# First head pair of the second attention set moved between the bias steps, last layer wholly in block form

## The chip, the cores and the metric

One core of one Trainium2 chip runs the whole program. The time is the device time of one execution in microseconds (us); a profile is one such execution, taken by the hardware profiler. The engines are PE (matrix products, into eight PSUM banks), DVE, ACT and POOL (element by element work; POOL reaches SBUF only) and SP, whose queue issues every DMA here.

## The reference

Attention with a bias made by a small network from positions, then a mixture of four experts over the tokens, then one more two-layer block. All is float32.

```
scores = q @ k.T / sqrt(64)                         # 2 batches, 8 heads, 576 positions
x = log1p(|i - j|) / log1p(max(i, 1))
bias = relu(x * w1 + b1) @ w2                       # 32 hidden units, 8 heads
attn = softmax(scores + bias); y = attn @ v         # tokens: 1152 x 512
out1 = sum_e p_e * (relu(y @ w1_e) @ w2_e)          # e = 0..3, 512 -> 1024 -> 512
h = out1 @ w_in; out = (h * cos(h)) @ w_out         # 512 -> 2048 -> 512
```

## The kernel before

The kernel is written as a list of steps, each with an engine, a duration, the steps it depends on and buffers by class. A planner (`Graph.order`) runs once on the host: it takes the steps in the order of their priorities as engines and buffers come free in its own count of time, and so fixes the order of every engine's queue. On the chip each queue then runs strictly in that order, and an instruction waits by semaphore only for the data and the buffers that it needs. The priorities are the order of writing, shifted by offsets (`O_...`) and by a list of seeds, `MOVES`; `P_...` say how much later an alternative engine may take a step.

Buffer classes that matter here: E (14 tiles of 128x640, named es: keys, values and scores of the first set, bias rows, score tiles), F (fs, 128x512), K (ks, split keys, queries and values), P1 (four single PSUM banks, p_153 to p_156) and P2 (two pairs of PSUM banks, p_160 and p_161).

The stages, in the order of writing:

- **Bias.** 36 steps (`bias_step`), each for 16 query positions and all 8 heads. Four operations on DVE or ACT make the hidden values (line 495 or 493), PE reduces them (line 506), DVE or ACT takes the result out (513 or 511), and SP stores it in DRAM (`biasD`), for steps of the mirrored part in a reversed copy too (line 524 on ACT, 525 on POOL; `biasR`). A step is 384, 448, 512 or 576 columns wide; one of 576 takes a P2 pair, the others a P1 bank.
- **First set** (`first_set`), the first 64 query positions, after four bias steps: for each head pair p = 0..3 and each batch b keys and values are loaded into E tiles, PE makes the scores (line 663), DVE adds the bias row and takes the minimum (617), ACT the exponential (620), POOL normalises (630), PE transposes (647, 650) and multiplies with the values (672).
- **Second set** (`second_set`), the other 512 positions, written after all 36 bias steps. Here products are split in a high and a low float32r part. `prep_pair` loads keys, queries and values of a pair and splits them: the high part on POOL or ACT (lines 538, 539), the low part on POOL or DVE (540). Each score product (line 699, 12 matmuls) fills both P2 pairs, one for each head; two minima, exponentials and normalisations follow, transposes, and products with the values (719). A pair p has four parts: two halves g of the positions by two batches, each with two score products. The bias tile of a score product is loaded from DRAM and serves both batches.
- **Fill** (`fill`, lines 1026, 1034): expert layers on the first 128 tokens, which the planner puts between the steps of the second set.
- **Experts** on the other 1024 tokens, mostly in block form (`block_products`, line 907): each 2x2 block product of 8 products is done with 7, on sums of blocks that DVE makes before. Token sums (`block_tokens`) are made of tokens that were stored in DRAM (`x1D`, `x2D`) and loaded again. Second layers are line 786, transposes of the result line 996.
- **Last layer**, in four chunks c of 512 hidden units. With `PLAIN = 1` chunk 0 is done directly (line 777) for all 1152 tokens, chunks 1 to 3 directly for the first 384 and in block form for the other 768. Its weights are split into parts during the expert stage (`singles`, `quads`), stored in DRAM and loaded again.

Of the kernel before, what the change touches and what calls it, by code (L numbers as in the profile page):

```python
# [36 lines left out]
    2173958, 2074786, 2643280, 8547416, 3098374, 2108113, 823829, 3486615, 5170615, 9452828,  # L37
    2633387, 6676825, 3992994,
# [234 lines left out]
def t_pool(n, ptr=0, two=False):  # L273
    return 145 + n * (2.11 if two else 0.86) + 80 * ptr
# [20 lines left out]
Q1 = S - Q0  # L295
# [8 lines left out]
NCONV, LATE, PLAIN = 2, 3, 1  # L304
# [5 lines left out]
NWAIT = 8  # L310
# [5 lines left out]
P_GEN, P_ADD, P_SPA, P_SPD, P_E32, P_REL, P_SUB, P_NRM, P_EV, P_REV, P_TWO = 200.0, 2500.0, 150.0, 1500.0, 300.0, 300.0, 2000.0, 3000.0, 3000.0, 50.0, 0.0  # L316

ON_ACT, P_HDV, P_HAC, P_EVD = ((36, (2, 3)),), 300.0, 150.0, 200.0

O_GEN, O_SGN, O_STT, O_ADD, O_SPL, O_EVC, O_NRM = 80, 80, -150, 0, 150, -10, 0  # L320

BAHEAD, HAHEAD, FAHEAD, BACK, BACK0, G_SET, G_FILL, G_MAIN = 7, 3, 2, 4, 2, 33, 6, 1
# [42 lines left out]
def build(ctx: ExitStack, tc: tile.TileContext, consts, q, v, qd, kp, vp, w12, probs, mw1, mw2, win, wout, out):  # L365
# [111 lines left out]
    bias_st, bias_mm = [], {}  # L477

    def bias_step(s, back, p2, gates=()):
# [9 lines left out]
        for t in range(4):  # L489
# [8 lines left out]
            G.step(*first, rd=rdt, wr=[(hid[t // 2], t)], after=gate, off=O_SGN if t in ts else O_GEN, port=True, alts=[(*other, wait)])  # L498
# [12 lines left out]
        G.step("ACT", t_act(W, 1), lambda: nc.scalar.activation(out=uo(), in_=pi(), func=AF.Copy, scale=nrec[:, s:s + 1]),  # L511
# [21 lines left out]
    x1_st, x2_st = {}, {}  # L533
    n_units = [0]
# [23 lines left out]
    def prep_pair(b, p, gate):  # L558

        kf, qf = Buf("E"), Buf("F")  # L560
        KH, KL, QH, QL = Buf("K"), Buf("K"), Buf("K"), Buf("K")
        dma(128 * S * 4, lambda: nc.sync.dma_start(out=kf.tile[:, :S], in_=kp[b, p]), wr=[kf], after=gate)
# [50 lines left out]
    def unit(bt, sp, es, i, out, tail, used):  # L613
# [3 lines left out]
        low = G.step("DVE", t_dve(S) + 10, lambda: nc.vector.tensor_tensor_reduce(  # L617
# [8 lines left out]
        G.step("DVE", 80, lambda: nc.vector.reciprocal(out=stats[:, 3, c:c + 1], in_=stats[:, 2, c:c + 1]), rd=[(st, "t")], wr=[(st, "r")])  # L626
# [56 lines left out]
    def second_set(p, gates):  # L683
# [3 lines left out]
        for g, b in ((g, b) for g in range(2) for b in range(B)):  # L687
# [15 lines left out]
            for hh in range(2):  # L703
# [20 lines left out]
                G.step("DVE", t_dve(256) + 40, lambda bank=bank, xt=xt, m0=m0, g=g, x32=x32: nc.vector.tensor_tensor(  # L724
# [3 lines left out]
            if g:  # L728
                whole(p, b, x32)

    def whole(p, b, x32):
        cs = slice(B * Q0 + Q1 * b, B * Q0 + Q1 * b + Q1)
        x1_st[p, b] = dma(128 * Q1 * 4, lambda: nc.sync.dma_start(out=x1D[p, :, Q1 * b:Q1 * b + Q1], in_=x32.tile[:, :Q1]), rd=[x32])
        G.step("ACT", t_act(Q1, 0, 1), lambda: nc.scalar.activation(out=xh[:, p, cs], in_=x32.tile[:, :Q1], func=AF.Copy),
               rd=[x32], wr=[(fix("xh"), (p, b))])
        sub = lambda e: e.tensor_tensor(out=xl[:, p, cs], in0=x32.tile[:, :Q1], in1=xh[:, p, cs].bitcast(F32), op=ALU.subtract)
        G.step("POOL", t_pool(Q1, 0, True), lambda: sub(nc.gpsimd), rd=[x32, (fix("xh"), (p, b))], wr=[(fix("xl"), (p, b))],
               alts=[("DVE", t_dve(Q1), lambda: sub(nc.vector), P_SUB)], port=True)
# [4 lines left out]
    for b, qs in enumerate(qss):  # L743
        dma(128 * 512 * 4, lambda b=b, qs=qs: nc.sync.dma_start(out=qs.tile[:, 0:512], in_=qd[b]), wr=[qs], after=[bias_mm[b, 0]])
# [43 lines left out]
    def run_ff(jobs, evac1, evac2, xr, final=None):  # L788
# [28 lines left out]
        l2(*todo.pop(0))  # L817
# [8 lines left out]
    def block_tokens(cols, keys, n, whole, stored, after, names=("xh", "xl"), t4n="t4"):  # L826
# [4 lines left out]
        def block(d):  # L831
            def load(dd, c):
                b = Buf("F")
# [19 lines left out]
            two(v22, v22, v12, ALU.subtract, [b22, b12], [b22], n, after=x)  # L853
            keep_("T2", v22, b22)

            two(v21, v21, v22, ALU.subtract, [b21, b22], [b21], n)
# [39 lines left out]
    def block_products(A, T_, n, evac, mid=None):  # L896
# [56 lines left out]
    def block_job(e, f0, cols, T_, n, gate, last):  # L953
# [3 lines left out]
        hbs = block_products(A, T_, n, moe_ev1)  # L957
# [382 lines left out]
```

## Time and profile before

| | |
|---|---|
| three runs, median (lowest to highest) | 778.99 us (778.15 to 780.88) |
| profiled execution: its time / its span | 780.83 / 779.0 us |
| PE busy | 761.4 us (98%), 4310 matmuls |
| DVE / ACT / POOL busy | 633.9 / 452.3 / 127.7 us |
| mean granted clock of PE | 0.989 |

The span runs from the first to the last instruction. PE's busy time counts a matmul from its start to the modelled end, so that overlapping ones make a full row even when each is slow. The granted clock says which share of full speed PE had.

### The profile page before, as it was taken

Reading aid. Unit: us, or ns where it says so; the run is one execution under the profiler, and the core shown is the slowest. Engines: PE = TensorE matmul, PEld = TensorE weight load, DVE = VectorE, ACT = ScalarE, POOL = GpSimd, SP = SyncE. Lnnn points to the kernel's source line nnn. Section 1 sums busy time; section 2 is a strip of 40 time slices with the busy share of each in tenths; the row PEclk is TensorE's granted clock in tenths of the full one; section 3 lists DMA queues with packets and bytes.
Section 4 is the critical chain, followed back from the end, with each engine's and each line's share of the span. In section 5 each row is a group of like instructions: output and inputs, shape, how many; then the busy total and the mean of one; then the engine's idle time right before and its main releaser. Section 6 shows DMA issues by size and latency. Waiting matters only on the chain.

```text
span 779.0 us, 13118 instructions
## 1 busy us (share of the span) xinstructions
PE 761.4 (98%) x4310; PEld 624.8 (80%) x4310; DVE 633.9 (81%) x1507; ACT 452.3 (58%) x950; POOL 127.7 (16%) x177
## 2 busy tenths in 40 slices
PE   9898799999999999999999999999999999999998
PEld 5445687887877888888888888888889899999987
DVE  7895687888786986979697979899979959986573
ACT  8885687878776545354445544544547647564440
POOL 0134575756637000000000000000000000000000
PEclk9999699999999999999999999999999999999999
DMA  6799966676728336162615644627594578462212
GB/s 196 234 302 296 300 206 220 193 237 198 232 60 288 133 121 213 49 201 79 229 42 162 218 148 136 211 99 231 187 302 147 185 267 286 151 221 82 77 59 95
DMA packets 94516, 142.00 MB, mean 182 GB/s; under 512 B 11505, under 2 KB 42865, under 8 KB 94449
## 3 DMA queue, kind: packets, MB, share of 16 engines
q1 hardware_dynamic: 94448, 141.17, 55.9%
q8 instruction: 34, 0.56, 0.3%
q14 instruction: 34, 0.27, 0.1%
HBM read 101.05 MB, written 40.08 MB: 181 GB/s over the span
## 4 chain that ended last, share of the span: by engine, by line
PE 76%; DVE 1%; ACT 1%; issue 0%
PE p L786 23%; PE p L907 18%; PE p1x L786 12%; PE p L777 7%; PE p1x L907 5%; PE p1x L777 3%; PE p L719 2%; PE p L1034 2%; PE p L647 1%; PE p L1026 1%; PE p L699 1%; PE p L996 1%; PE p1x L1026 0%; DVE ht L712 0%; DVE es L617 0%; DVE hs L551 0%
## 5 line engine op out<-in xcount | busy, mean ns | idle before, releaser
L786 PE MATMUL p<-wx,hs 128*128 128x512 f32 x804 | 188.5, 390 | 0.0
L786 PEld LDWEIGHTS p<-wx,hs 128*128 128x128 f32 x804 | 150.3, 188 | 31.2
L786 PE MATMUL p1x<-wx,hs 128*128 128x512 f32 (+1 forms) x408 | 93.9, 383 | 0.0
L786 PEld LDWEIGHTS p1x<-wx,hs 128*128 128x128 f32 x408 | 75.0, 188 | 14.8
L630 POOL TENSOR_SCALAR es<-es,stats 128x576 f32<-128x576 f32 (+2 forms) x104 | 64.7, 637 | 71.4 <-DVE stats L626 22.8
L907 PE MATMUL p<-xh,wx 128*128 128x512 f32 (+1 forms) x236 | 76.4, 374 | 0.0
L907 PE MATMUL p<-tx,wx 128*128 128x512 f32 (+1 forms) x294 | 69.4, 373 | 0.0
L620 ACT ACTIVATE es<-es,stats 128x576 f32<-128x576 f32 x72 | 55.4, 770 | 15.7 <-DVE stats L617 15.0
L617 DVE CUSTOM_DVE_ANT_0 es<-p,es 128x576 f32<-128x576 f32 x72 | 52.6, 750 | 12.3 <-DMA es<-biasD 5.5
L907 PEld LDWEIGHTS p<-tx,wx 128*128 128x128 f32 x294 | 54.1, 188 | 8.2
L539 ACT ACTIVATE wx<-fs 128x512 fp32r<-128x512 f32 (+1 forms) x71 | 41.2, 600 | 26.2 <-DVE fs L823 20.2
L540 DVE TENSOR_TENSOR wx<-fs,wx 128x512 fp32r<-128x512 f32 (+1 forms) x67 | 44.2, 676 | 12.7 <-ACT wx L539 12.5
L551 DVE TENSOR_TENSOR hs<-p,hs 128x512 fp32r<-128x512 f32 x64 | 43.5, 688 | 10.2 <-ACT hs L549 9.1
L777 PE MATMUL p<-xh,wx 128*128 128x384 f32 (+1 forms) x184 | 51.5, 351 | 0.0
L647 PEld LDWEIGHTS p<-ident,es 128*128 128x128 f32 x288 | 34.0, 145 | 20.0 <-issue 9.2
L647 PE MATMUL p<-ident,es 128*128 128x128 f32 x288 | 46.1, 287 | 3.7 <-POOL es L630 2.8
L907 PEld LDWEIGHTS p<-xh,wx 128*128 128x128 f32 x236 | 44.0, 188 | 6.8
L987 DVE SCALAR_TENSOR_TENSOR fs<-p,prob,fs 128x512 f32<-128x512 f32 x47 | 35.0, 745 | 17.2 <-PE p L786 15.5
L907 PE MATMUL p<-xl,wx 128*128 128x512 f32 (+1 forms) x118 | 44.2, 374 | 0.0
L495 DVE TENSOR_SCALAR bs<-cst,cpos 128x576 f32<-128x576 f32 (+3 forms) x98 | 41.7, 487 | 1.4 <-PE p L506 1.2
L699 PE MATMUL p<-ks,ks 64*128 64x288 f32 x384 | 36.1, 322 | 6.6 <-DVE stats L617 5.0
L539 ACT ACTIVATE fs<-fs 128x256 fp32r<-128x256 f32 x45 | 18.4, 415 | 40.3 <-DVE fs L1098 40.1
(198 smaller groups left out, 1544.5 us busy)
## 6 DMA issues: line engine op xcount, KB each, us to landing
fs<-in_mw SPq DMA_DIRECT2D x113, 256.0 KB, 4.2
wx<-winhl SPq DMA_DIRECT2D x32, 256.0 KB, 4.8
wx<-wouthl SPq DMA_DIRECT2D x32, 256.0 KB, 4.5
wouthl<-fs SPq DMA_DIRECT2D x23, 256.0 KB, 2.4
winhl<-fs SPq DMA_DIRECT2D x22, 256.0 KB, 2.6
fs<-in_wout SPq DMA_DIRECT2D x22, 256.0 KB, 3.5
fs<-in_win SPq DMA_DIRECT2D x20, 256.0 KB, 3.9
es<-in_kp SPq DMA_DIRECT2D x16, 288.0 KB, 4.6
```

What stands on the lines that cost most here:

```text
L495: dve = ("DVE", t_dve(W, 1, True), lambda w0=w0, u=u, t=t: nc.vector.tensor_scalar(out=hv(t), in0=tab[:, w0:w0 + W], scalar1=cpos[:, u:u + ...
L539: act = ("ACT", t_act(n, 0, 1), lambda: nc.scalar.activation(out=hv(), in_=fv(), func=AF.Copy))
L540: low = lambda e: e.tensor_tensor(out=lv(), in0=fv(), in1=hv().bitcast(F32), op=ALU.subtract)
L551: G.step("DVE", t_dve(n) + 25, lambda: nc.vector.tensor_tensor(out=dst(AL), in0=src(), in1=dst(AH).bitcast(F32), op=ALU.subtract), rd=[ps_ ...
L617: low = G.step("DVE", t_dve(S) + 10, lambda: nc.vector.tensor_tensor_reduce(out=f3(e.tile[:, :S]), in0=sp.tile[:, :, 0:288], in1=f3(bt.til ...
L620: exp_all.append(G.step("ACT", t_act(S, 1, 1) + 124, lambda: nc.scalar.activation(out=e.tile[:, :S], in_=e.tile[:, :S], func=AF.Exp, scale ...
L630: nrm = lambda g: g.tensor_scalar(out=dst(), in0=src(), scalar1=rs, scalar2=1.0, op0=ALU.mult, op1=ALU.mult)
L647: nc.tensor.transpose(tp.tile[:, 128 * kt:128 * kt + 128], e.tile[:, 128 * kt:128 * kt + 128], ident)
L699: nc.tensor.matmul(out=o[hh], lhsT=x.tile[ls, c:c + 128], rhs=y.tile[ls, cols], start=(i == 0), stop=(i == 2))
L777: nc.tensor.matmul(out=z.tile[:, 0:n], lhsT=w[dt][2][wi]()[:, 128 * ft:128 * ft + 128], rhs=x[:, dt, p0:p0 + n], start=(dt == 0 and i == 0 ...
L786: nc.tensor.matmul(out=y.tile[:, 0:m], lhsT=hx, rhs=w[ft][2][wi]()[:, c0:c0 + m], start=(ft == 0 and i == 0), stop=(ft == nf - 1 and i == 2))
L907: nc.tensor.matmul(out=z.tile[:, 0:n], lhsT=x()[:, 128 * t:128 * t + 128], rhs=y(), start=(start and d == 0 and i == 0), stop=(d == 1 and ...
```

## The change

- **Order of writing.** The first pair's second set (p = 0) is now begun after 24 bias steps: `second_set` became a generator that stops after each of its four parts, `BIAS_AT = 24, 30, 36` puts its first part behind step 24, the second behind step 30 and the third behind step 36.
- **Keys and values.** The first set takes the pairs in the order 1, 2, 3, 0, and the E tiles of pair 0 are kept (`raw`), so that `prep_pair` splits them from there. Two loads of keys and four of values go away; the values' tile has another layout, which the splits read with a stride. The first loads of the first set wait for the first hidden values only (`EARLY`).
- **Last layer.** `PLAIN = 0`: chunk 0 too is done directly for 384 tokens and in block form for 768. Its weights now also need the block sums (stores and loads of `s12`, `s34`). The experts' second layers end with token tiles 3, 4, 1, 2 and no longer in falling order; the parts of tiles 6 to 8 that only the direct form read are no longer written.
- **The planner's numbers.** New seeds, offsets, waits and a few durations; more of the hidden values go to ACT (59 instead of 46), fewer to DVE (85 instead of 98).
- New branches for `NHALF = 0` are not taken (`NHALF = 1`), and `direct` stays empty.

```
 MOVES = (
-    2173958, 2074786, 2643280, 8547416, 3098374, 2108113, 823829, 3486615, 5170615, 9452828,
...
+    7995270, 9512881, 659327, 8807516, 3479167, 4347581, 5230207, 3159208, 2587635, 4906331,
...
-NCONV, LATE, PLAIN = 2, 3, 1
+NCONV, LATE, PLAIN = 2, 3, 0
...
-NWAIT = 8
+NWAIT = 4
+
+SHARE, EARLY, QEARLY = 1, 1, 0
+
+BIAS_AT = 24, 30, 36
...
-ON_ACT, P_HDV, P_HAC, P_EVD = ((36, (2, 3)),), 300.0, 150.0, 200.0
...
+ON_ACT, P_HDV, P_HAC, P_EVD = ((8, (2, 3)), (36, (3,))), 50.0, 50.0, 200.0
...
     def prep_pair(b, p, gate):
 
-        kf, qf = Buf("E"), Buf("F")
+        had = raw.get((p, b))
+        kf, qf = had[0] if had else Buf("E"), Buf("F")
         KH, KL, QH, QL = Buf("K"), Buf("K"), Buf("K"), Buf("K")
-        dma(128 * S * 4, lambda: nc.sync.dma_start(out=kf.tile[:, :S], in_=kp[b, p]), wr=[kf], after=gate)
+        if not had:
+            dma(128 * S * 4, lambda: nc.sync.dma_start(out=kf.tile[:, :S], in_=kp[b, p]), wr=[kf], after=gate)
...
-            vf, V = Buf("F"), Buf("K")
+            vf, V = had[1] if had else Buf("F"), Buf("K")
...
         kf, vf, at, bank = Buf("E"), Buf("E"), Buf("E"), Buf("P1")
+        if p < SHARE:
+            raw[p, b] = kf, vf
...
             head_end.append(qk_all[-1])
             if g:
                 whole(p, b, x32)
+            yield
...
-    for p in range(4):
+    for p in (*range(SHARE, 4), *range(SHARE)):
         shared = None
         for b in range(B):
-            shared = first_set(p, b, qss[b], [bias_mm[NSTEP0 - 2, 0]] + head_end[-FAHEAD:1 - FAHEAD], shared)
+            gate = hid0[:1] if len(head_end) < EARLY else [bias_mm[NSTEP0 - 2, 0]]
+            shared = first_set(p, b, qss[b], gate + head_end[-FAHEAD:1 - FAHEAD], shared)
...
-    for s in range(NSTEP0, 36):
-        bias_step(s, BACK, False)
+    made = NSTEP0
     for p in range(4):
-        second_set(p, [bias_mm[G_SET, 0]])
+        for n in BIAS_AT if p == 0 else ():
+            while made < n:
+                bias_step(made, BACK, False)
+                made += 1
+            if n == BIAS_AT[0]:
+                parts = second_set(p, [bias_mm[G_SET, 0]])
+            next(parts)
+        for _ in parts if p == 0 else second_set(p, [bias_mm[G_SET, 0]]):
+            pass
...
-            for j in range(n // 128) if c or not last else reversed(range(n // 128)):
+            for j in range(n // 128) if c or not last else reversed(range(n // 128)) if PLAIN else (2, 3, 0, 1):
...
+            d0 = 2 if t >= 6 and not PLAIN else 0
```

PE's queue where the first set ends and the second begins. Before: the last transposes and value product of the first set (lines 647, 650, 672) are followed at once by score products of the second set (line 699), all bias steps being done.

```order
L506 MATMUL p_161<-bs_146,prm 32x288 x2
L672 MATMUL p_155<-es_131,es_139 128x128 x5
L647 MATMUL p_153<-ident,es_129 128x128 x4
L650 MATMUL p_156<-ident,es_129 64x128
L672 MATMUL p_156<-es_129,es_142 128x128 x5
L699 MATMUL p_161<-ks_117,ks_119 128x288
L699 MATMUL p_160<-ks_117,ks_119 128x288
...
L699 MATMUL p_160<-ks_118,ks_119 128x288
L699 MATMUL p_161<-ks_118,ks_119 128x288
L647 MATMUL p_156<-ident,es_142 128x128 x4
```

After, at the same place (the same operations are now lines 657, 660, 684, 711 and, for the bias, 512; 1058 is the fill's first layer):

```order
L657 MATMUL p_155<-ident,es_136 128x128 x4
L660 MATMUL p_154<-ident,es_136 64x128
L684 MATMUL p_153<-es_142,es_129 128x128 x5
L684 MATMUL p_154<-es_132,es_135 128x128 x5
L711 MATMUL p_161<-ks_117,ks_125 128x288
...
L512 MATMUL p_154<-bs_147,prm 32x448 x2
...
L512 MATMUL p_160<-bs_151,prm 32x288 x2
...
L512 MATMUL p_155<-bs_147,prm 32x448 x2
...
L1058 MATMUL p_154<-x_80,fs_98 128x128
L711 MATMUL p_161<-ks_117,ks_125 128x288
```

Eleven bias steps have moved behind the first score product: four of 448 columns and seven of 576 (printed as 288, in two halves). Eight of them, and the fill's first layer, stand before the second score product, the last three before the third.

POOL's queue at the splits of pair 0. Before, they (lines 538, 540) follow the last normalisation of the first set (line 630):

```order
L630 TENSOR_SCALAR es_131<-es_131,stats 128x576
L630 TENSOR_SCALAR es_129<-es_129,stats 128x576
L538 TENSOR_SCALAR ks_117<-es_137 128x576
L540 TENSOR_TENSOR ks_118<-es_137,ks_117 128x576
L538 TENSOR_SCALAR ks_119<-fs_99 128x512
```

After, they (lines 544, 546) stand among normalisations (line 640) and reversed copies (531):

```order
L640 TENSOR_SCALAR es_140<-es_140,stats 128x576
L544 TENSOR_SCALAR ks_117<-es_136 128x576
L544 TENSOR_SCALAR ks_119<-es_129 128x5x64
L546 TENSOR_TENSOR ks_118<-es_136,ks_117 128x576
L640 TENSOR_SCALAR es_142<-es_142,stats 128x576
L640 TENSOR_SCALAR es_132<-es_132,stats 128x576
L546 TENSOR_TENSOR ks_120<-es_129,ks_120 128x5x64
L531 TENSOR_SCALAR fs_101<-es_141 128x222
```

From the first normalisation to the last split of a query, POOL has 24 instructions in the new order: 8 normalisations, 4 splits of keys (2 high, 2 low) and 12 shorter ones.

PE's queue where the last layer begins. Before, the last transposes of the experts' result (line 996) are followed by the direct products of chunk 0 (line 777), 96 in all:

```order
L996 MATMUL p_153<-ident,fs_111 128x128 x4
L777 MATMUL p_154<-xh,wx_3160 128x384
...
L996 MATMUL p_153<-ident,fx_2854 128x128 x4
L777 MATMUL p_156<-xh,wx_3160 128x384
```

After (transposes 1026, block products 937, direct products 803):

```order
L1026 MATMUL p_155<-ident,fs_112 128x128 x4
...
L1026 MATMUL p_155<-ident,fs_113 128x128 x4
L937 MATMUL p1x_2710<-xh,wx_2750 128x384
...
L1026 MATMUL p_153<-ident,fs_109 128x128 x4
L937 MATMUL p_156<-xh,wx_2750 128x384
...
L803 MATMUL p_153<-xh,wx_2750 128x384
...
L937 MATMUL p_153<-tx_2991,wx_3151 128x384
```

Eighteen block products that read tokens directly, and 48 direct ones, now stand between the last transposes of a blocked tile and the first block product that reads a token sum (tx).

## Rows read from the trace of the kernel before

**Rows 1.** The head of the page, and PE's part of its first section.

```profile
span 779.0 us, 13118 instructions
...
PE 761.4 (98%) x4310; PEld 624.8 (80%) x4310; DVE 633.9 (81%) x1507; ACT 452.3 (58%) x950; POOL 127.7 (16%) x177
```

**Rows 2.** Busy time by stretches: length, engines, granted clock, DMA share, GB/s.

```profile
25.00:35.00 10.00, 7.20 (x54) 3.86 (x54) 7.34 (x22) 8.02 (x17) 2.45 (x4) 0.83 0.62 204
70.00:75.00 5.00, 4.36 (x37) 3.08 (x29) 1.25 (x5) 1.56 (x3) 3.11 (x4) 1.00 0.86 274
75.00:80.00 5.00, 1.74 (x13) 1.17 (x12) 0.23 (x1) 2.01 (x5) 4.24 (x6) 0.74 0.93 290
80.00:85.00 5.00, 2.29 (x15) 2.02 (x16) 2.85 (x9) 2.40 (x6) 3.63 (x4) 0.50 0.92 281
85.00:90.00 5.00, 4.36 (x25) 3.71 (x24) 3.85 (x14) 3.02 (x7) 1.73 (x3) 0.50 0.83 295
90.00:95.00 5.00, 5.00 (x44) 4.55 (x45) 3.75 (x14) 3.33 (x10) 2.96 (x6) 0.90 0.92 263
95.00:250.00 155.00, 152.52 (x1198) 125.28 (x1195) 126.24 (x363) 120.18 (x272) 98.85 (x137) 1.00 0.65 205
256.00:776.00 520.00, 519.99 (x2444) 446.37 (x2443) 430.95 (x938) 259.62 (x529) 0.00 (x0) 1.00 0.49 160
```

**Rows 3.** PE in order of time: start, length, instructions, idle before and releaser.

```profile
29.96 1.12 PE L647 MATMUL p<-ident,es 128*128 128x128 f32 x4 [2.80 <-POOL es L630]
...
48.14 1.71 PE L506 MATMUL p<-bs,prm 128*32 128x448 f32 x16
...
60.38 2.15 PE L506 MATMUL p<-bs,prm 128*32 128x288 f32 x32
...
73.43 1.57 PE L672 MATMUL p<-es,es 128*128 128x128 f32 x10 [0.64 <-ACT es L555]
75.39 0.40 PE L699 MATMUL p<-ks,ks 64*128 64x288 f32 x2 [0.39 <-POOL ks L538]
77.05 1.33 PE L699 MATMUL p<-ks,ks 64*128 64x288 f32 x10 [1.25 <-POOL ks L540]
82.71 1.81 PE L699 MATMUL p<-ks,ks 64*128 64x288 f32 x12 [4.33 <-DVE stats L617]
```

**Rows 4.** DVE in order of time: first minimum, a run of hidden values, second set.

```profile
26.33 0.76 DVE L617 CUSTOM_DVE_ANT_0 es<-p,es 128x576 f32<-128x576 f32 x1 [1.54 <-DMA biasD<-es]
...
52.06 2.64 DVE L495 TENSOR_SCALAR bs<-cst,cpos 128x576 f32<-128x576 f32 x6
...
81.01 0.76 DVE L617 CUSTOM_DVE_ANT_0 es<-p,es 128x576 f32<-128x576 f32 x1 [5.49 <-DMA es<-biasD]
```

**Rows 5.** POOL in order of time: normalisations, then the splits of the keys.

```profile
29.15 1.58 POOL L630 TENSOR_SCALAR es<-es,stats 128x576 f32<-128x576 f32 x2
...
52.33 2.98 POOL L630 TENSOR_SCALAR es<-es,stats 128x576 f32<-128x576 f32 x1 [0.28 <-ACT bs L493]
...
66.67 0.75 POOL L630 TENSOR_SCALAR es<-es,stats 128x576 f32<-128x576 f32 x1 [6.95 <-DVE stats L626]
...
72.20 0.68 POOL L538 TENSOR_SCALAR ks<-es 128x576 fp32r<-128x576 f32 x1 [0.52 <-DMA es<-in_kp]
72.96 1.40 POOL L540 TENSOR_TENSOR ks<-es,ks 128x576 fp32r<-128x576 f32 x1
```

**Rows 6.** DMA issues from 60 to 82 us: count, size, median us to landing.

```profile
es<-in_kp SPq DMA_DIRECT2D x2, 288.0 KB, 4.4
...
es<-biasD SPq DMA_DIRECT2D x2, 256.0 KB, 4.8
```

**Rows 7.** The chain that ended last: start, length, pieces; last layer.

```profile
582.71 0.44 PE p L996 x4
...
641.55 2.08 PE p L907 x12
```

**Rows 8.** DMA issues from 560 to 600 us, the tokens stored and loaded again.

```profile
x2D<-fs SPq DMA_DIRECT2D x6, 256.0 KB, 2.8
...
fs<-x2D SPq DMA_DIRECT2D x5, 192.0 KB, 3.6
```

More of the change, by code (lines that the diff above doesn't have):

```diff
@@ L273, in t_pool @@
 def t_pool(n, ptr=0, two=False):
-    return 145 + n * (2.11 if two else 0.86) + 80 * ptr
+    return (170 if two else 145) + n * (2.11 if two else 0.86) + 90 * ptr
 def t_col(n):
@@ L497, in bias_step @@
             first, other, wait = (act, dve, P_HDV) if t in ts else (dve, act, P_HAC)
-            G.step(*first, rd=rdt, wr=[(hid[t // 2], t)], after=gate, off=O_SGN if t in ts else O_GEN, port=True, alts=[(*other, wait)])
+            x = G.step(*first, rd=rdt, wr=[(hid[t // 2], t)], after=gate, off=O_SGN if t in ts else O_GEN, port=True, alts=[(*other, wait)])
+            hid0.append(x)
         pb = Buf("P1" if npc == 1 else "P2")
@@ L510, in bias_step @@
         pi = lambda: pb.tile[:, :, 0:m] if npc == 2 else pb.tile[:, 0:m]
-        G.step("ACT", t_act(W, 1), lambda: nc.scalar.activation(out=uo(), in_=pi(), func=AF.Copy, scale=nrec[:, s:s + 1]),
+        G.step("ACT", t_act(W, 1) + 20, lambda: nc.scalar.activation(out=uo(), in_=pi(), func=AF.Copy, scale=nrec[:, s:s + 1]),
                rd=[pb, (cb, "r1")], wr=[(u_, 0)], off=O_STT,
@@ L616, in unit @@
         n_units[0] += 1
-        low = G.step("DVE", t_dve(S) + 10, lambda: nc.vector.tensor_tensor_reduce(
+        low = G.step("DVE", t_dve(S) + 25, lambda: nc.vector.tensor_tensor_reduce(
             out=f3(e.tile[:, :S]), in0=sp.tile[:, :, 0:288], in1=f3(bt.tile[:, :S]), scale=-0.125, scalar=BIG,
@@ L824, in two, with block_tokens @@
         return G.step("DVE", t_dve(n), lambda: f(nc.vector), rd=rd, wr=wr, port=True, **kw)
-    def block_tokens(cols, keys, n, whole, stored, after, names=("xh", "xl"), t4n="t4"):
+    def block_tokens(cols, keys, n, whole, stored, after, names=("xh", "xl"), t4n="t4", had={}):
         c0, c1 = cols
@@ L832, in load @@
             def load(dd, c):
+                if (dd, c) in had:
+                    b = had[dd, c][0]
+                    return b, (lambda: b.tile[:, 0:n])
                 b = Buf("F")
@@ L998, in moe_ev2 @@
             cs = slice(128 * t, 128 * t + 128)
-            G.step("ACT", t_act(512), lambda: nc.scalar.activation(out=xh[:, :, cs], in_=f3(tp.tile, 4), func=AF.Copy),
+            d0 = 2 if t >= 6 and not PLAIN else 0
+            m = 128 * (4 - d0)
+            G.step("ACT", t_act(m), lambda: nc.scalar.activation(out=xh[:, d0:4, cs], in_=f3(tp.tile, 4)[:, d0:4], func=AF.Copy),
                    rd=[tp], wr=[(fix("x2h"), t)])
@@ L1004, in moe_ev2 @@
                     out=x2D[:, :, 128 * t - 384:128 * t - 256].rearrange("a p n -> p a n"), in_=f3(a(), 4)), rd=[acc[t]])
-            G.step("DVE", t_dve(512), lambda: nc.vector.tensor_tensor(
-                out=xl[:, :, cs], in0=f3(tp.tile, 4), in1=xh[:, :, cs].bitcast(F32), op=ALU.subtract),
+            G.step("DVE", t_dve(m), lambda: nc.vector.tensor_tensor(
+                out=xl[:, d0:4, cs], in0=f3(tp.tile, 4)[:, d0:4], in1=xh[:, d0:4, cs].bitcast(F32), op=ALU.subtract),
                 rd=[tp, (fix("x2h"), t)], wr=[(fix("x2l"), t)])
```

63 lines of the change are left out of this document (36 added, 27 removed).

## The prediction

> **What bounds the kernel now.** I read the head of the page first: PE is busy 761.4 of 779.0 us [rows 1], so whatever shortens the kernel must either fill PE's holes or take work from PE. The table by stretches shows where which holds [rows 2]. From 256 us on PE is busy 519.99 of 520 us at a granted clock of 1.00: nothing gets faster there except by fewer matmuls. From 95 to 250 us it is busy 152.52 of 155. Ahead of that lie two holes. Busy time times granted clock is the time that the same work would take at full speed; by that measure the stretch from 25 to 35 us does 7.20 x 0.83 = 6.0 us of work in 10 and loses 4.0 us. The five stretches from 70 to 95 do 4.36 + 1.29 + 1.15 + 2.18 + 4.50 = 13.5 us of work in 25 and lose 11.5 us. Of these 11.5, 7.2 us are idle time (25 minus 17.75 busy) and 4.3 us are matmuls at the lower of the two clock levels (1.2 instead of 2.4 GHz), where the clock fell after PE had been idle and stayed through 80 to 90. Each us of idle time cost about 0.6 us more in clock.
>
> PE's instructions in order of time say what the holes wait for [rows 3]. In the first, transposes of the first set wait 2.80 us for POOL's normalisation; behind that stands DVE's first minimum, which had waited 1.54 us for a DMA [rows 4]. The second begins at 75.0 (73.43 + 1.57), when the first set and the bias are finished. The first score products of the second set wait 0.39 and 1.25 us for the splits, which POOL started at 72.20 when the keys landed: 0.68 + 1.40 us [rows 5]. Then PE waits 4.33 us for DVE's minimum, since the two PSUM pairs are full, and that minimum waits 5.49 us, until 81.01, for its bias tile from DRAM [rows 4]. The tile's load takes 4.8 us [rows 6] while the DMA engines are 0.92 to 0.93 busy [rows 2]. So the second hole is a pipeline that starts cold: load, split, product, load, minimum, with nothing else for PE to do.
>
> **The change, term by term.** The sum is made against the profiled execution, 780.83 us (span 779.0 and 1.83 around it). The median of the runs is 778.99, 1.84 lower; I carry the difference over unchanged.
>
> *Cover for the second hole.* Eleven bias steps now stand behind the first score product. Two steps of 448 columns take 1.71 us, two of 576 take 2.15 [rows 3]: 4 x 0.855 + 7 x 1.075 = 10.9 us of PE work, placed where PE waits today, against a hole of 11.5 us. It is the same work as before, so what is gained is the hole, not the work. The keys and values of the first part need no load: two loads of 288 KB and four of 160 KB go, 1.2 MB, or 4.2 us of DMA at the 290 GB/s of 75 to 80 us. At best both holes vanish: -15.5 us. From this I subtract new waits.
>
> - *First hole.* It has the same cause, and the new order only puts another score product and bias step ahead of the transposes and issues the first loads earlier. Bounds: 0.5 us (a few short waits) to 4.0 (unchanged). I take 2.
> - *Splits in time.* PE reaches the first score product of the second set about 10.9 us earlier, and 2 us earlier again for the first hole: 75.0 - 12.9 = 62. POOL by then must have done 24 instructions from its first normalisation at 29.15: 8 normalisations of 0.75 = 6.0, four key splits 2 x (0.68 + 1.40) = 4.2, 12 shorter ones at about 0.5 (between 0.2 and 0.7, scaled by columns from 0.68) = 6.0; together 16.2 us, with 33 us to do them in [rows 5]. Yet where DVE ran six hidden-value operations in a row (52.06 to 54.70 [rows 4]), a normalisation took 2.98 us instead of 0.75 [rows 5]. DVE has 37 such operations in that time, 37 x 2.64/6 = 16.3 us at most. If the two engines exclude each other altogether, the end is 29.15 + 16.2 + 16.3 = 61.7, just PE's 62. Bounds 0 and 5 us; I take 1.
> - *Second bias tile.* The E tile for the second score product's bias row comes free only at the last transposes of the first set, and its load takes 4.8 us [rows 6]; bias steps of 576 columns then miss the held PSUM pair. Bounds 0 and 3, taken 1.5, since eight bias steps lie between.
> - *DVE between the first and third score product.* It still makes hidden values there, against some 11 us of bias work and two score products of about 2 us on PE. Bounds 0 and 4 (the 4.33 wait), taken 1.
> - *Bias tiles of the last steps.* A store and a load stand between the last bias steps and the minima that read them, 2.8 and 4.8 us by the nearest rows [rows 6, 8]; bounds 0 and 3, taken 1.
> - *Clock.* Only a long idle piece costs it; bounds 0 and 3, taken 0.
>
> New waits: 2 + 1 + 1.5 + 1 + 1 = 6.5. First part: -15.5 + 6.5 = -9.0 us.
>
> *Last layer.* Chunk 0 in block form needs 36 products more on token sums, 32 fewer on xh and 16 fewer on xl: 12 matmuls of 384 columns fewer, and twelve take 2.08 us [rows 7]. That is paid in full, where PE is never idle: -2.1.
>
> *Its start.* Before, 96 direct products covered the way of the last experts' tokens through DRAM; now the first product on a token sum comes earlier. Between the transposes of the last blocked tile and that product PE has a second-layer group (12 x 512 columns, 2.08 x 512/384 = 2.8), two transposes (0.44 each [rows 7]), 18 block products (3.1) and 48 direct ones (8.3): 15.1 us. The way: store 2.8, load 3.6 [rows 8], and about five DVE or ACT operations no longer than the 0.76 of a minimum [rows 4]: 10.2. Slack 5; bounds of the wait 0 and 3, taken 0.3. The sums `s12` and `s34` add 16 transfers of about 256 KB and some 26 operations on DVE, hidden by a DMA share of 0.49 and by DVE's 431 of 520 us [rows 2]; without that cover the transfers alone would cost 4.2 MB at 160 GB/s, 26 us.
>
> *95 to 250 us.* The second set's other pairs are reordered by the seeds alone; 2.5 us are idle there, so 0, between -2 and +2.
>
> Sum: -9.0 - 2.1 + 0.3 = -10.8; 780.83 - 10.8 = 770.0 for an execution like the profiled one, 768.2 for the median.
>
> **Rivals.**
>
> *Nearly all of it comes back (762).* Every new wait at its low bound: -15.5 + 0.5 - 2.1 = -17.1. For it: 10.9 us of cover against 11.5 of loss, and the splits no longer wait for a load. Against it: five waits at their bounds at once.
>
> *The shared port (775).* POOL's splits lag behind DVE's hidden values, by the 2.98 for 0.75 us. The first score product is then 5 us late instead of 1, and the clock falls for 3 us: -10.8 + 4 + 3 = -3.8. Against it: DVE makes fewer hidden values than before (85 operations, not 98), and POOL has 33 us for 16. The Trainium skill, "SBUF — State Buffer", section "SBUF: two separate sides", says that DVE and GpSimd share a pair of ports as an exclusive lock, held for one whole instruction. By that rule a POOL instruction would wait at most for the one DVE operation in progress, 0.44 us here, some 10 us over 24 instructions, and the splits would be in time. The trace agrees that one blocks the other; the row is harsher than the rule: the normalisation waited out a run of operations, not one.
>
> *Bound by DMA, the hole only moves (777).* In 70 to 95 us the DMA engines are 0.83 to 0.93 busy, and only 1.2 MB (4.2 us) leaves. Were the bias tiles late for that reason in the new order as well, 4.2 of the 11.5 us and the 2.1 of the last layer would come back, and waits at the interleaved steps of some 4 us would eat most of it: 777. Against it: the transfers now spread over a longer stretch, since the bias stores no longer end before the second set begins.
>
> *Slower (784).* PE's queue is strict: the first score product of the second set stands ahead of eleven bias steps that were ready without it. If it is late, they all are; each us is paid in full, with 0.6 on top when the clock falls as it did after 75 us. The forecast's 10.8 is eaten, and 2.3 us beyond, at (10.8 + 2.3)/1.6 = 8 us of lateness more, i.e. if POOL's 16.2 us and the DVE work that excludes it stretch by a quarter (32.5 to 41). At 10 us: -10.8 + 16 = +5. For it: a row in which POOL took four times its time. Against it: it would have to be so for most of the stretch.
>
> **Numbers.** Forecast (764 to 773) 0.55; nearly all back 0.20; shared port 0.12; bound by DMA 0.07; slower 0.06. 0.3%, or 2.3 us, is about what runs of this kernel can tell from no change. Faster: 0.55 + 0.20 + 0.12 = 0.87; same 0.07; slower 0.06. The range 760 to 777 leaves out the last case, half of the one bound by DMA and about 0.05 below; the likeliest case's own is 764 to 773.
>
> **What would show it.** Right: PE starts the first second-set score product (now line 711) near 62 us, has no wait over 2 us from 60 to 95, and the granted clock is 1.00 there; 12 matmuls of 384 columns fewer; the first product on a token sum (937) waits under 0.5 us. Wrong: a wait of line 711 for POOL of several us with the clock falling behind it; a wait of DVE's minimum for biasD as long as the 5.49; a hole at the start of the last layer; or a first hole as wide as before.

## The result and the profile after

The changed kernel takes 765.69 us (median of 4 runs, 765.42 to 766.26); the kernel before took 779.36 in the same comparison (4 runs). The ratio is 0.9825, interval 0.9806 to 0.9843: 13.7 us faster. The forecast was 768.2, in a range of 760 to 777. The profiled execution takes 765.42 us, its span is 763.6. It lies 0.27 us below its median, where the one of before lies 1.5 above its own, so the two traces differ by 1.7 us more than the medians do.

The head of the page and PE's part of its first section, to hold against [rows 1]:

```profile
span 763.6 us, 13117 instructions
...
PE 754.7 (99%) x4298; PEld 619.9 (81%) x4298; DVE 644.9 (84%) x1520; ACT 457.2 (60%) x962; POOL 124.7 (16%) x180
```

There are 12 matmuls fewer, and PE is idle 8.9 us instead of 17.6. The same stretches as in [rows 2], with length, PE, PEld, DVE, ACT, POOL, granted clock, DMA share and GB/s:

```profile
25.00:35.00 10.00, 9.71 (x81) 6.62 (x73) 7.32 (x23) 7.92 (x21) 3.37 (x6) 1.00 0.75 248
70.00:75.00 5.00, 4.37 (x43) 3.46 (x36) 3.97 (x12) 4.03 (x8) 2.21 (x4) 1.00 0.71 258
75.00:80.00 5.00, 5.00 (x62) 3.35 (x63) 4.31 (x11) 4.84 (x11) 1.71 (x3) 1.00 0.96 310
80.00:85.00 5.00, 5.00 (x51) 4.21 (x43) 2.29 (x6) 2.50 (x6) 0.00 (x0) 1.00 0.95 306
85.00:90.00 5.00, 5.00 (x25) 2.65 (x25) 3.84 (x14) 2.88 (x8) 1.73 (x3) 1.00 0.89 302
90.00:95.00 5.00, 5.00 (x45) 4.30 (x45) 4.35 (x13) 3.24 (x8) 1.86 (x4) 1.00 0.90 299
95.00:250.00 155.00, 153.45 (x1173) 126.85 (x1172) 135.96 (x372) 122.69 (x277) 94.56 (x130) 1.00 0.65 206
256.00:760.00 504.00, 504.00 (x2371) 432.99 (x2370) 424.81 (x925) 255.01 (x524) 0.00 (x0) 1.00 0.52 172
```

Both holes are gone, and the clock stays at its higher level throughout. Counted as in the prediction (length less busy time times granted clock), 25 to 35 us now loses 0.3 us instead of 4.0, 70 to 95 loses 0.6 instead of 11.5, and 95 to 250 loses 1.6 instead of 2.5.

PE in order of time where the second set begins, to hold against [rows 3]:

```profile
59.52 1.03 PE L711 MATMUL p<-ks,ks 64*128 64x288 f32 x11
60.48 5.52 PE L512 MATMUL p<-bs,prm 128*32 128x448 f32 x54
66.28 0.94 PE L512 MATMUL p<-bs,prm 128*32 128x448 f32 x2 [0.28 <-DVE bs L500]
67.63 2.90 PE L512 MATMUL p<-bs,prm 128*32 128x288 f32 x40 [0.42 <-ACT es L517]
70.46 1.16 PE L1058 MATMUL p<-x,fs 128*128 128x128 f32 x8
72.25 1.06 PE L711 MATMUL p<-ks,ks 64*128 64x288 f32 x12 [0.63 <-DVE es L519]
...
73.74 1.06 PE L1058 MATMUL p<-x,fs 128*128 128x128 f32 x8
...
78.51 1.06 PE L1058 MATMUL p<-x,fs 128*128 128x128 f32 x8
79.49 1.18 PE L512 MATMUL p<-bs,prm 128*32 128x288 f32 x16
80.60 1.16 PE L1058 MATMUL p<-x,fs 128*128 128x128 f32 x8
...
84.93 1.98 PE L1066 MATMUL p<-fs,fs 128*128 128x512 f32 x4
86.85 1.07 PE L711 MATMUL p<-ks,ks 64*128 64x288 f32 x12
87.84 1.12 PE L1066 MATMUL p<-fs,fs 128*128 128x512 f32 x2
```

The first score product runs from 59.3 to 60.5, and the waits behind it are 0.28, 0.42 and 0.63 us. But the reader should see a second kind of work between the score products, which the prediction did not price: the fill's two layers (lines 1058 and 1066). From 70 to 95 us they take 6.4 + 4.1 = 10.5 us of PE; before, the fill had 2.75 us there.

The DMA issues from 45 to 70 us say where its weights come from (size, count, median us to landing). After, and below it before:

```profile
fs<-in_mw SPq DMA_DIRECT2D x6, 256.0 KB, 4.4
...
fs<-in_q SPq DMA_DIRECT2D x2, 256.0 KB, 2.9
```

```profile
es<-in_kp SPq DMA_DIRECT2D x4, 288.0 KB, 4.6
es<-in_vp SPq DMA_DIRECT2D x3, 320.0 KB, 4.5
```

After, six loads of fill weights (in_mw) have been issued by 70 us; before, none, and DMA was still busy with keys and values, all but one of these loads being the first set's.

DVE's first minimum and POOL's normalisations among the splits, to hold against [rows 4, 5]:

```profile
22.13 0.75 DVE L627 CUSTOM_DVE_ANT_0 es<-p,es 128x576 f32<-128x576 f32 x1
```

```profile
47.31 0.87 POOL L544 TENSOR_SCALAR ks<-es 128x576 fp32r<-128x576 f32 x1 [0.99 <-DMA es<-in_kp]
48.26 1.41 POOL L546 TENSOR_TENSOR ks<-es,ks 128x576 fp32r<-128x576 f32 x1
...
52.19 1.07 POOL L640 TENSOR_SCALAR es<-es,stats 128x576 f32<-128x576 f32 x1 [0.21 <-DVE stats L636]
...
54.71 1.39 POOL L544 TENSOR_SCALAR ks<-fs 128x512 fp32r<-128x512 f32 x2 [0.42 <-DMA fs<-in_q]
```

The first minimum no longer waits and comes 4.2 us earlier. The last key split ends at 49.7 and the last query split at 56.1, 3 us before PE needs them.

### The profile page after: what moved, and what is told of

The parts are those of the page before. It is cut to its first block, busy times and chain, and to the rows that moved or that the text cites. A ratio compares the mean times of both kernels' runs of the same rounds, so it can differ in the third digit from the quotient of the medians.

```text
span 763.6 us, 13117 instructions
## 1 busy us (share of the span) xinstructions
PE 754.7 (99%) x4298; PEld 619.9 (81%) x4298; DVE 644.9 (84%) x1520; ACT 457.2 (60%) x962; POOL 124.7 (16%) x180
## 4 chain that ended last, share of the span: by engine, by line
PE 90%; DVE 4%; ACT 2%; DMA 2%; issue 1%; POOL 0%; SPq 0%; DVEq 0%; ACTq 0%
PE p L812 22%; PE p L937 19%; PE p1x L812 14%; PE p1x L937 7%; PE p L803 5%; PE p L731 4%; PE p L711 4%; PE p L657 4%; PE p L1066 4%; PE p L1058 3%; DVE bs L500 3%; PE p1x L803 2%; PE p L512 1%; DMA biasD<-es 1%; PE p L684 1%
## 5 line engine op out<-in xcount | busy, mean ns | idle before, releaser
L812 PE MATMUL p<-wx,hs 128*128 128x512 f32 (+1 forms) x756 | 177.0, 387 | 0.0
L812 PEld LDWEIGHTS p<-wx,hs 128*128 128x128 f32 x756 | 140.1, 188 | 28.2
L812 PE MATMUL p1x<-wx,hs 128*128 128x512 f32 x456 | 109.8, 390 | 0.0
L812 PEld LDWEIGHTS p1x<-wx,hs 128*128 128x128 f32 x456 | 85.4, 188 | 17.6
L937 PE MATMUL p<-xh,wx 128*128 128x512 f32 (+1 forms) x252 | 80.5, 371 | 0.0
L555 ACT ACTIVATE hs<-p 128x512 fp32r<-128x512 f32 x62 | 35.9, 593 | 9.2 <-PE p L657 8.5
L512 PE MATMUL p<-bs,prm 128*32 128x288 f32 (+3 forms) x384 | 39.6, 486 | 1.8 <-DVE bs L500 0.9
L498 ACT ACTIVATE bs<-cst,cpos 128x576 f32<-128x576 f32 (+3 forms) x59 | 37.9, 700 | 2.2 <-DVE cst L465 1.9
L803 PE MATMUL p<-xh,wx 128*128 128x384 f32 (+1 forms) x128 | 37.5, 356 | 0.0
L731 PE MATMUL p<-hs,ks 128*128 128x256 f32 x248 | 36.9, 293 | 0.5 <-DVE ht L724 0.5
```

The lines of the kernel that those rows point to most:

```text
L498: act = ("ACT", t_act(W, 1, 1), lambda w0=w0, u=u, t=t: nc.scalar.activation(out=hv(t), in_=tab[:, w0:w0 + W], func=AF.Relu, bias=cpos[:, ...
L512: nc.tensor.matmul(out=pv(a)[32 * t:32 * t + 32], lhsT=wpad, rhs=hv(t, m * a, m), start=True, stop=True, tile_position=(0, 32 * t))
L731: nc.tensor.matmul(out=bank.tile[:, 256:512], lhsT=V.tile[:, 128 * kt:128 * kt + 128], rhs=m, start=(i == 0), stop=(i == 8))
L803: nc.tensor.matmul(out=z.tile[:, 0:n], lhsT=w[dt][2][wi]()[:, 128 * ft:128 * ft + 128], rhs=x[:, dt, p0:p0 + n], start=(dt == 0 and i == 0 ...
L812: nc.tensor.matmul(out=y.tile[:, 0:m], lhsT=hx, rhs=w[ft][2][wi]()[:, c0:c0 + m], start=(ft == 0 and i == 0), stop=(ft == nf - 1 and i == 2))
L937: nc.tensor.matmul(out=z.tile[:, 0:n], lhsT=x()[:, 128 * t:128 * t + 128], rhs=y(), start=(start and d == 0 and i == 0), stop=(d == 1 and ...
```

## The experiments

All medians are set against the kernel before on the same chip. "Lost" is PE time lost from 60 to 95 us, worked out as above from seven windows; "fill" is the PE time of the fill's two layers from 70 to 95 us; "weights" is the number of fill weight loads issued from 45 to 70 us.

| run | median us | ratio, interval | lost | fill | weights |
|---|---|---|---|---|---|
| before | 779 | 1 | 11.5 | 2.8 | 0 |
| changed | 765.7 | 0.983 (0.981 to 0.984) | 1.4 | 10.5 | 6 |
| changed, again | 766.0 | 0.984 (0.982 to 0.986) | 1.2 | 10.5 | 6 |
| changed, chunk 0 done directly | 771.1 | 0.989 (0.987 to 0.991) | 1.6 | 9.6 | 6 |
| bias steps first | 769.4 | 0.987 (0.985 to 0.989) | 3.8 | 9.1 | 4 |
| keys and values loaded again | 771.8 | 0.990 (0.988 to 0.993) | 5.1 | 4.3 | 0 |
| both of the last two | 774.3 | 0.993 (0.991 to 0.995) | 8.1 | 1.1 | 0 |
| EARLY = 0 | 774.1 | 0.995 (0.994 to 0.997) | 5.5 | 3.0 | 0 |
| fill held back | 777.5 | 0.998 (0.997 to 1.000) | 7.8 | 0 | 0 |
| fill held back, bias steps first | 777.9 | 0.999 (0.998 to 1.000) | 11.6 | 0 | 0 |
| before, fill's first weights early | 786.1 | 1.008 (1.006 to 1.010) | 11.8 | 9.5 | 8 |
| before, two groups' weights early | 796.6 | 1.022 (1.020 to 1.024) | 11.0 | 10.5 | 8 |
| changed, no seeds | 773.0 | 0.992 (0.990 to 0.995) | 5.5 | 3.6 | 0 |
| changed, fill's first weights early | 768.5 | 0.986 (0.984 to 0.987) | 3.8 | 6.4 | 8 |

**Chunk 0 done directly again.**

```diff
-NCONV, LATE, PLAIN = 2, 3, 0
+NCONV, LATE, PLAIN = 2, 3, 1
```

> The changed kernel with chunk 0 of the last layer done directly again (PLAIN = 1); all queues up to the experts are as in the changed kernel. Theory: the block form pays its 12 matmuls in full, so this kernel is 2.1 us slower than the changed one, 767.8 us, or 767.5 if the start of the last layer waits 0.3 us in block form. Rival: the start of the block form, or its extra sums and transfers, give it back; then 765.7, the same as the changed kernel.

Measured: 771.12 us (0.989, 0.987 to 0.991), 5.1 more than the changed kernel's repetition: neither of the two that were expected. The stretches say why. It has 12 matmuls more, and PE is idle for 1.88 us between 250 and 550, where it waits twice for DVE and ACT at a block product:

```profile
PE p L937 <- ACT fs L944: 1.0, 1, 1.0
PE p L937 <- DVE fs L947: 0.9, 1, 0.9
```

That is a part whose queues differ from the changed kernel's. The first 25 us lost 3.6 us instead of 1.3, in the same order on every engine; the two traces' first minima are at 23.81 and 22.13. So the 2.1 us of the 12 matmuls, taken from their price and not measured alone, are one of three pieces of the 5.1, and the two others belong to the experts' order and to the start; the difference of the medians alone does not measure the block form.

**Bias steps first; keys and values loaded again; both.**

```diff
-BIAS_AT = 24, 30, 36
+BIAS_AT = 36,
```

```diff
-SHARE, EARLY, QEARLY = 1, 1, 0
+SHARE, EARLY, QEARLY = 0, 1, 0
```

> The changed kernel with the second set begun only after all 36 bias steps (BIAS_AT = 36); the first pair's keys and values are still kept from the first set. Theory (the bias steps are cover for a cold pipeline): the second hole is back with its wait for the bias tile, only without the wait for the keys; 8 to 10 us slower than the changed kernel, 774 to 776 us, with PE idle for several us behind the first second-set score product and the granted clock down at 0.5 to 0.8 there. Rival (the kept keys and values did it): at most 3 us slower, under 769. Rival (the planner's new numbers did it): at most 4 us slower, under 770.

> The changed kernel with the first pair's keys and values loaded again for the second set (SHARE = 0), still begun between the bias steps. Theory of cover: the loads fit beside the bias steps; 0 to 2 us slower, 765.7 to 768. Rival (the 1.2 MB of loads count in a stretch with the DMA engines 0.75 to 0.99 busy): 4 us or more slower, 770 or above, with the first second-set score product waiting for POOL's splits and these for the keys.

> The changed kernel with both undone (second set after all 36 bias steps, keys and values loaded again); the planner's numbers and the last layer are those of the changed kernel. Theory: the gain of the first part is gone: 776 to 779 us, the kernel before less the 2.1 of the last layer. Rival (the planner's numbers did it): under 771.

Measured: 769.44, 771.81 and 774.29. The first result contradicts the prediction's own mechanism, by which 774 to 776 was expected. All bias steps stand ahead of the second set, as before the change, and still only 3.8 us are lost from 60 to 95 and the clock never falls: the fill has taken the bias steps' place (9.1 us of it). Loading keys and values again costs more than undoing the move of the bias steps, and not by a wait for the splits: no fill weight is issued before 70 us, and PE stalls in short waits up to 85 us. But this run takes away more than the kept tiles. In its order the first score product of the second set runs at 68.5 us instead of 59.3, and only 4.5 us of bias products stand behind it instead of 10.9. The run with both undone, expected at 776 to 779, is not the order of before either: two bias steps still stand behind the first score product. It loses 8.1 us, all of it idle time in waits of at most 1.14 us, at a granted clock of 1.00, and 5 us of the gain are left.

**The changed kernel again, and EARLY = 0.** The first has no edit; the second is

```diff
-SHARE, EARLY, QEARLY = 1, 1, 0
+SHARE, EARLY, QEARLY = 1, 0, 0
```

> The changed kernel once more, beside the next three. With chunk 0 done directly, the first 25 us lost 2.3 us more than in the changed kernel though every queue is the same up to there; DVE's first minimum came at 23.81 instead of 22.13 us, after a DMA. If that is the chip or the hour, this run shows it too: 767 to 768 us, the minimum after 23 us. If it belongs to the program, this run is as the first: 765.4 to 766.3 us, the minimum at 22.1.

> The changed kernel with the first loads of the first set no longer allowed to start with the first hidden values (EARLY = 0); the planner then orders the first set anew. Theory (early loads close the first hole): 2.5 to 4 us of PE time lost between 20 and 35 us come back, 768 to 770. Rival (the order of score products and bias steps closes it): 1 us or less, 766.7 at most, unless the new order costs elsewhere.

Measured: 766.03 (765.23 to 766.80) and 774.12. The repetition's first minimum came at 22.76, between the two others, and its first 25 us lost 2.4. So the start differs by about 1 us between two executions of one program; the 3.6 of the run with chunk 0 done directly lie 1.2 above the higher of the two. With EARLY = 0 the stretch from 25 to 35 us loses 0.31 us, as little as with it: the early loads do not close the first hole. The 8 us come from elsewhere, since the planner gave everything behind a new order: from 60 to 95 us 5.5 are lost instead of 1.2, with the fill late once more and the first score product at 68.1. The rest is not placed; this trace is of an execution 1.7 us below its median.

**The fill held back, with the bias steps moved and without.**

```diff
-BAHEAD, HAHEAD, FAHEAD, BACK, BACK0, G_SET, G_FILL, G_MAIN, G_TOK = 8, 3, 4, 4, 3, 15, 5, 1, 1
+BAHEAD, HAHEAD, FAHEAD, BACK, BACK0, G_SET, G_FILL, G_MAIN, G_TOK = 8, 3, 4, 4, 3, 15, 8, 1, 1
```

> The changed kernel with the expert layers on the first 128 tokens (the fill) held back until the second set's first part is under way (G_FILL = 8); up to the first second-set score product PE's queue is unchanged, and the bias steps still stand behind it. Theory (bias steps are the cover): within 2 us of the changed kernel, 765.7 to 768. Rival (the fill is the cover, as the run with all bias steps first suggests, in which the fill's products stood where PE would wait): 5 us or more slower, 771 or above.

> Both covers taken away: all 36 bias steps ahead of the second set, and the fill held back (G_FILL = 8); keys and values of the first pair are still kept. If cover of either kind is what closes the second hole, it is back here as in the kernel before, less the wait for the keys: 8 to 11 us slower than the changed kernel, 774 to 777, with the granted clock below 1 between 70 and 95 us. Rival (kept keys and values alone close it): 769 to 771, as with the bias steps first and the fill early.

Measured: 777.53, where the rival won, and 777.85, just above the 774 to 777 expected. With the bias steps where the change puts them, keys and values kept and the first score product at 59.3 us, almost nothing of the gain is left once the fill is late. PE's rows of the first of the two show where most of it goes:

```profile
71.05 1.18 PE L512 MATMUL p<-bs,prm 128*32 128x288 f32 x16 [0.49 <-ACT es L517]
...
77.80 1.06 PE L711 MATMUL p<-ks,ks 64*128 64x288 f32 x12 [0.84 <-ACT es L517]
80.49 1.05 PE L711 MATMUL p<-ks,ks 64*128 64x288 f32 x12 [1.63 <-DVE stats L627]
82.00 0.66 PE L657 MATMUL p<-ident,es 128*128 128x128 f32 x4 [0.46 <-POOL es L640]
83.14 1.07 PE L711 MATMUL p<-ks,ks 64*128 64x288 f32 x12 [0.48 <-DVE stats L627]
84.14 0.66 PE L657 MATMUL p<-ident,es 128*128 128x128 f32 x4
84.63 0.27 PE L660 MATMUL p<-ident,es 128*128 128x128 f32 x1
84.74 0.60 PE L657 MATMUL p<-ident,es 128*128 128x128 f32 x4
85.92 1.06 PE L711 MATMUL p<-ks,ks 64*128 64x288 f32 x12 [0.58 <-DVE stats L627]
88.08 1.83 PE L731 MATMUL p<-hs,ks 128*128 128x256 f32 x8 [1.10 <-DVE ht L724]
```

and DVE's between them:

```profile
78.99 0.76 DVE L627 CUSTOM_DVE_ANT_0 es<-p,es 128x576 f32<-128x576 f32 x1 [2.04 <-PE p L711]
...
79.67 0.75 DVE L627 CUSTOM_DVE_ANT_0 es<-p,es 128x576 f32<-128x576 f32 x1
```

Up to 77 us the bias steps cover PE, but for waits under half a us. Then score products follow one another: each takes 1.06 us and fills both PSUM pairs, and the next waits until two minima of 0.76 have emptied them. Between them stand only a few transposes, 0.7 us at 82 and 1.2 from 84.1, and the first value products come at 88.08. PE is idle 5.1 us from 75 to 90, and the granted clock is 0.83 from 85 to 95. Of the 5.1, 3.5 are waits on the PSUM pairs (0.84, 1.63, 0.48, 0.58); the others are for POOL's normalisation (0.46) and for DVE's part of a value product (1.10). DVE itself waits for PE (2.04) at the first minimum; no load is late. Only other work for PE covers such waits, and the fill is that work.

The hole is not the whole price. Against the changed kernel's repetition the medians differ by 11.5 us and the traces by 9.7, while from 60 to 95 us 6.5 more are lost. The other 3 us of the traces are not placed; they may belong to the order that the planner made for a later fill.

In the second run the wait of the second score product is as long, and DVE's first minimum waits for PE and no longer for its bias tile:

```profile
76.31 1.45 PE L711 MATMUL p<-ks,ks 64*128 64x288 f32 x12 [1.00 <-ACT es L517]
79.33 1.81 PE L711 MATMUL p<-ks,ks 64*128 64x288 f32 x12 [1.57 <-DVE stats L627]
```

```profile
77.83 0.76 DVE L627 CUSTOM_DVE_ANT_0 es<-p,es 128x576 f32<-128x576 f32 x1 [3.76 <-PE p L711]
```

Yet 11.6 us are lost, as before the change, and the clock falls to 0.50. Here 4.1 us of the idle time lie ahead of the first score product, in waits of 0.8 to 1.3 for DVE and ACT at the bias steps. The two runs' loss differs by 3.8, of which 1.4 is idle time and the rest clock; the two traces differ by 2.1 us and the medians by 0.3. So how much the moved bias steps save without the fill stays open.

**Before, with only the fill moved.** The first group's weight loads get an earlier priority (in a second kernel, with `< 2`, those of two groups), and `G_FILL`, the number of the first set's score product that the fill's first loads wait for, goes from 6 to 3.

```diff
-                    out=w.tile[:, 0:512], in_=src), wr=[ws[i]], after=gate, keep=FKEEP)
+                    out=w.tile[:, 0:512], in_=src), wr=[ws[i]], after=gate, keep=0 if 2 * e + c < 1 else FKEEP, off=-1000 if 2 * e + c < 1 else 0)
...
-BAHEAD, HAHEAD, FAHEAD, BACK, BACK0, G_SET, G_FILL, G_MAIN = 7, 3, 2, 4, 2, 33, 6, 1
+BAHEAD, HAHEAD, FAHEAD, BACK, BACK0, G_SET, G_FILL, G_MAIN = 7, 3, 2, 4, 2, 33, 3, 1
```

> The kernel before, with one thing changed: the loads of the fill's first group get an earlier priority, so that its 16 first-layer row groups and 4 second-layer ones (about 4.4 and 4.1 us of PE work) stand between the first set's end and the second score product of the second set. No bias step is moved, keys and values are loaded again, the last layer is as before. Theory (fill work standing where PE waits is what closes the second hole): 5 to 8 of the 11.5 us lost between 70 and 95 us come back, 771 to 774. Rival (its 2 MB of weights take 7 us of the same busy DMA engines, so all loads behind them come later and the hole moves): 777 to 780.

> The kernel before with the loads of the fill's first two groups made earlier: a second such block stands before the third score product. Theory of the fill as cover: at least as fast as with one group, 769 to 773. Rival (DMA): 4 MB more ahead of the bias tiles, slower than with one group by 3 us or more.

Measured: 786.05, and 796.61 (1.022, 1.020 to 1.024). The first is 6.8 us slower than the kernel before, beyond both ranges that were expected, on the rival's side; the second is slower still, as the rival had it. The fill alone is no remedy. Its 9.5 us stand in the hole, and 11.8 us are lost all the same. The windows of the run with one group (columns as above), then SP's row at the first load of the second set, and below it the same load in the kernel before:

```profile
70.00:75.00 5.00, 2.44 (x14) 1.64 (x12) 1.31 (x5) 1.66 (x4) 0.22 (x1) 0.92 1.04 400
75.00:80.00 5.00, 3.88 (x15) 3.15 (x15) 0.28 (x1) 0.60 (x1) 1.13 (x2) 0.50 0.92 307
```

```profile
75.81 0.33 SPq L562 DMA_DIRECT2D es<-in_kp  x1
```

```profile
68.70 0.33 SPq L562 DMA_DIRECT2D es<-in_kp  x1
```

The DMA engines are 0.96 busy from 60 to 70 us and 1.04 from 70 to 75, and the keys of the second set are issued 7.1 us later than before. From 45 us to that issue DMA moved 7.53 MB in the kernel before (to 69) and 9.72 here (to 76), at a busy share of 0.94 in both: the 2.2 MB more are about what the eight loads of weights carry, 2.1. PE waits 3.15 us, until 75.6, for a normalisation of the first set, and works at the lower clock level behind it. The figures fit weights that push later loads back by the time that they take themselves; in the changed kernel, 1.2 MB of keys and values are no longer loaded.

**No seeds.** The changed kernel with an empty `MOVES`.

> The changed kernel with an empty list of seeds: order of writing, kept keys and values, block form and all other numbers as changed. In its order 46 of 48 groups of bias products still stand before the first second-set score product, and the fill begins only behind the fourth. Theory (what counts is what PE's queue holds at the second hole, not the order of writing): most of the first part's gain is missing, 774 to 778. Rival (order of writing and kept tiles do it): 766 to 769.

Measured: 772.98, a little below the 774 expected, with 46 of 48 groups of bias products ahead of the second set's first product. So the order of writing did not move the bias steps by itself; the planner moved them only with the seeds, and with them it brought the fill forward too. What is faster than before without them is the last layer, 2.4 us in the first hole (1.7 lost instead of 4.0) and 6 us from 60 to 95; 1.9 us are given back between 95 and 250.

**After, with the fill's first weights earlier** (the same edit as in the kernel before).

> The changed kernel with the loads of the fill's first group made earlier, as in the kernel before with one group: 12 of its 16 first-layer row groups then stand among the bias steps ahead of the first second-set score product. If PE's waits from 50 to 75 us (about 2.5 us lost) are still to be covered: 764 to 765.5. Rival (no cover is missing any more; the loads only crowd the DMA engines there): 766 to 769.

Measured: 768.46, slower by 2.4 us than the repetition. With eight weights instead of six issued before 70 us, waits for bias work of 1.3 and 1.4 us appear. No experiment beats the changed kernel.

## Why the prediction came out right, point by point

- **What bounds it, and the two holes.** Right: nearly all the time came from PE's two holes and from 12 matmuls; PE is idle for nothing from 256 us on, as before. Lost time fell from 20.1 to 5.8 us in the whole trace. With the 2.1 of the last layer that is 16.4 against 15.4 by the spans; the 1.0 left over lies in busy time that is not dense, and I can't place it. The medians give 13.7, since the profiled execution of before took 1.5 us more than its median; the difference carried over was 1.84, and between the two traces 1.7 was measured.
- **Cover for the second hole.** This is the step that failed, though its sum did not. The prediction put eleven bias steps, 10.9 us, against a hole of 11.5 that it took for a cold start alone, "with nothing else for PE to do". For the kernel before that reading holds: its waits for the splits and for the bias tile, 0.39, 1.25 and 4.33, make 6.0 of the 7.2 us of idle time [rows 3]. But another wait stands behind this one. While the later stages are still empty, the score products must hand over two PSUM pairs through DVE's minima; with the keys there and the bias steps where the change puts them, PE is idle 5.1 us from 75 to 90 for that in the main, and the first of these waits is as long with all bias steps ahead (1.63 and 1.57). In PE time from 60 to 95 us: 11.6 lost with neither cover, 7.8 with bias steps only, 3.8 with the fill only, 1.4 with both. By these, the fill is worth 6 to 8 us, the bias steps 2 to 4; by the medians, 8 to 11.5 and 0.3 to 3.4. These sizes belong to their orders: the run without seeds loses 5.5 with 3.6 us of fill and one bias step behind the first score product. The order's rows in the section on the change showed the fill's first layer ahead of the second score product, and the prediction passed over it. That the sum came out 2.5 us from the median all the same is luck in this term: the fill paid for much of what the bias steps were to pay.
- **Keys and values.** The 1.2 MB were priced as 4.2 us of DMA time and then not used in the sum. They are what the fill's early weights are paid with: with the loads back, no weight comes before 70 us, and the median rises by 6.1 us against the first measurement. That the freed time is what lets the weights in is argued from the issues and from the kernel before with early weights, whose loads were 7.1 us late; the runs with the loads back have other queues in other places too, with the first score product 9 us later.
- **First hole.** Taken as 2 us left, it is 0.3. EARLY is not needed for that, as the run without it showed. The load of the first bias tile is issued at 14.91 us instead of 18.08 and DVE's minimum no longer waits; that this order on SP's queue is the cause was not tried alone. Part of the 4.0 was the execution: with the same queues up to there, the two kernels with early weights lost 1.8 and 4.3.
- **Splits in time, the second bias tile, DVE between, last bias tiles.** Taken 4.5 together; 1.4 us are lost from 60 to 95, in waits of 0.28, 0.42 and 0.63. PE was at the first product at 59.3, not 62, and the splits were 3 us early. The bounds held, the values taken were too high.
- **Clock.** Taken 0, and it cost 0. The reason, that only a long idle piece costs it, does not hold as it stands: in the run without seeds no wait from 60 to 95 us is longer than 1.08 us, and the granted clock is 0.66 from 80 to 85; in the run with bias steps first and keys loaded again, waits of up to 1.14 us, 8.1 in all, cost none.
- **The shared port.** Wrong as a rival: POOL's normalisations take up to 1.07 us from 45 to 60 us, where one took 2.98 [rows 5]. That is near what the Trainium skill, "SBUF — State Buffer", section "SBUF: two separate sides", gives: a POOL instruction waits for the one DVE operation in progress. The trace after agrees, with 0.3 us above the 0.75; the 2.98, 2.99 and 2.58 in the kernels that keep the order of before do not, and no run tells why.
- **Last layer.** 12 matmuls fewer, 2.1 us by the price of twelve; no run measured it alone. PE is idle for nothing from 256 to 760 us, so the first product on a token sum waits for nothing; 0.3 was taken.
- **Slower, or bound by DMA.** The first product was early, so its price did not arise. DMA as a bound was given 0.07, and the time was not bound by it; but it limits what may be brought forward, as 786 and 796 us show.

## What to carry to other kernels

When a pipeline with few buffers starts, count two waits apart: the one for its first data, which earlier loads and work moved behind the first product remove, and the one from stage to stage while the later stages are still empty, which here only independent work covered. The second can hide behind the first and come out when that is gone. Look in the new order for everything that has come into the hole, not only for what the change names. Work that is to fill a hole brings its own loads; where the DMA engines are 0.9 busy, as here, free that much DMA time ahead of it, or look for what it will delay.

## What the runs showed of the hardware that was not expected

- The same kernel, with the same queues, has its first minimum at 22.13 or 22.76 us, and a kernel whose queues are the same until about 250 us had it at 23.81. There the loads of the bias tile took 6.3 us, against 4.4 and 4.3, and the minimum waited 1.59 us for DMA; in the run at 22.76 the first of these loads was issued 0.56 us later than in that at 22.13. What sets these differences is not shown.
- In the kernel before, two groups of early weights cost 17 us, of which 7.8 are idle PE time from 250 to 300 us, far from the place of the edit; PE waits there 4.7 us for DVE's parts of the last value products (line 712), at a granted clock of 0.83 in the first 10 us.
